# Sums of raw weights moved from VectorE to GpSimd in three sweeps, with a re-laid plan

## Chip, cores and metric

One core of one Trainium2 chip runs the whole program. The time is device microseconds of one execution; given are the median of several executions and, beside it, the one execution that the hardware profiler recorded. Engines: TensorE (PE, its weight loads PEld), VectorE (DVE), ScalarE (ACT), GpSimd (POOL), and SyncE (SP), which issues nearly all DMAs.

## What is computed

Attention over 4 sequences of 576 tokens with 8 heads of 64 (a causal window of 128 and a linear bias per head), then two layers of the same shape on the 2304 x 512 result, the first with an ELU, the second with a SiLU:

```python
scores = scale * q @ k.T + bias             # masked to 0 <= rel < 128
x = softmax(scores) @ v                     # reshaped to 2304 x 512
h = x @ w_in;  g = where(h > 0, h, exp(min(h, 0)) - 1);  x = g @ w_out     # 512 -> 2048 -> 512
h = x @ w_in2; g = h * (1 / (1 + exp(-h)));              out = g @ w_out2
```

The weights arrive as 64-bit floating-point numbers, two 32-bit words each.

## The kernel before

**Stages.** The first stage (to about 200 us) is attention, interleaved with the first quarter of the first layer's hidden width (`block_first`, `hidden`, `output_first`). The second stage, `layers()`, runs 21 steps. A step is one of three blocks of 768 tokens in one sweep; a sweep is four tiles `f` of 128 hidden columns (`SWEEPS`), three sweeps in the first layer and four in the second. A step multiplies in (`quad`, matmuls at L1254) and multiplies out (`seven_outputs`, matmuls at L1420).

**By seven.** Both products of a step are done on 2 x 2 blocks with seven block products instead of eight (Winograd's scheme), which asks for sums and differences of blocks, on the activations and on the weights. Every operand is split into a rounded upper part (a copy on ACT) and a remainder (a subtraction on DVE), and each product is three matmuls.

**Weights.** `weight(i)` prepares one tile of weights: a DMA of 512 KB into a raw buffer (a ring of four), ACT and DVE turn the two words into one 32-bit number (L471, L472, L476), and it lies in the `top` words; the `low` words are free from then on. For two neighbouring tiles (`f` odd closes the pair) four sums of 128 x 256 blocks are formed into the low words: s1 to s4 for `w_in` (L505) and t1 to t4 for `w_out` (`y_weight`, L434). After each two of them a `split_weight` follows, its ACT copy at L402 and its DVE remainder at L403. So one pair of tiles has four sums, one sweep has 2 pairs of each kind, 16 sums; the seven sweeps by seven have 112.

**Order.** Nothing is scheduled by hand. Each operation is handed to `Plan` with its engine, a cost in us, what it reads and writes, and sometimes a due time. `Plan.run` computes from the back how late each operation may start and then lays all of them in order of a simulated time: an engine that is free takes, of the operations that are ready, the most urgent. The instructions are emitted in that order, and on the chip each engine runs its own queue in that order, waiting on semaphores where an input is not there. Inputs to the simulation are constants: `DRAIN` (time from an engine's end to when others see it), `TURN` (a change of the kind of matmul), the costs, and `LATER`, by which a DMA is taken to land later than its size says. `SHAKES` is a list of (time, seed): from that simulated time on, a random choice of operations gets its urgency changed at random.

**Shared port.** `op.port` is true by default for operations on DVE and POOL, and the plan then lets only one such operation of the two engines run at a time. DVE operations that read PSUM are given `port=False`.

**POOL.** It scales softmax rows (L685, port true) and makes a few constants in the attention stage, and has nothing to do afterwards.

Of the kernel before, what the change touches and what calls it, by code (L numbers as in the profile page):

```python
# [18 lines left out]
P = 128  # L19
# [16 lines left out]
class Plan:  # L36

    LINK = 0.06
    SAME = {"DVE": 0.11, "ACT": 0.1}
    DRAIN = {"PE": 0.16, "ACT": 0.09, "DVE": 0.065, "POOL": 0.04}  # L40
    DMA_START, DMA_END = 1.2, 1.3
# [5 lines left out]
    SWITCH, STAY, EAGER = 0.1, (0.5, 4.0), 30.0  # L47
    TURN, RUN = 0.025, 1.1

# [119 lines left out]
def attention_elu_silu_kernel(  # L169
# [32 lines left out]
    for bi, (g0, n) in enumerate(blocks):  # L202
# [6 lines left out]
    NRAW = 4  # L209
    SCRATCH = {4: (1, 0), 5: (1, 1), 6: (1, 2), 7: (2, 0)}  # L210
    BIG = 6 * P
    HALF = BIG // 2
# [14 lines left out]
    BY_HAND = 4  # L227
    LATER = 0.9, 0.6, 0.4
    SHAKES = (
# [12 lines left out]

# [168 lines left out]
    def seven(layer, f):  # L411
        return any((layer, sw) in BY_SEVEN and f0 <= f < f1 for sw, (f0, f1) in enumerate(SWEEPS[layer]))

    def y_weight(t):

# [17 lines left out]
        def form(d, x, y):  # L433
            add("DVE", 0.34, lambda: nc.vector.tensor_tensor(d[0](), x[0](), y[0](), op=ALU.subtract), r=x[1] + y[1], w=d[1])  # L434
        src, r = whole(t, 1)
# [10 lines left out]
    def weight(i):  # L446
# [48 lines left out]
        else:  # L495
# [8 lines left out]
            def form(d, x, y, op):  # L504
                add("DVE", 0.34, lambda: nc.vector.tensor_tensor(d[0](), x[0](), y[0](), op=op), r=x[1] + y[1], w=d[1])  # L505
            split_weight(("wb", i), None, a22[0], None, w2, a22[1])
# [124 lines left out]
    def scores(u):  # L631
# [14 lines left out]
        def after():  # L646
            exps = []
            for j in range(2):
                for e in range(2):
                    g, i = 2 * t + e, 2 * j + e  # L650
                    c0 = first_col(g) // 2
                    b = pick.get(g, "bias")

                    def biased(j=j, e=e, i=i, c0=c0, b=b):
                        nc.vector.tensor_tensor_reduce(  # L655
                            T["p", u % 3][:, j, e, PAD + c0:PAD + WIDE], st(j)[:, e, c0:], T[b,][:, 2 * hp + j, c0:], -scale, 3.0e38,
                            ALU.add, ALU.min, T["neg", u % 4][:, i:i + 1])
                    pk = [("p", u % 3, j, e)] + ([("p", u % 3, "lo"), ("p", u % 3, "hi")] if u < 3 else [])
                    add("DVE", 0.29, biased, r=[sk[j], (b, 2 * hp + j)], w=pk[:1] + [("neg", u % 4, i)], port=False)

                    def exped(j=j, e=e, i=i, c0=c0):
                        dst = T["p", u % 3][:, j, e, PAD + c0:PAD + WIDE]
                        nc.scalar.activation(dst, dst, AF.Exp, bias=T["neg", u % 4][:, i:i + 1], scale=-1.0,  # L663
                                             accum_out=T["sm", u % MS][:, e, j:j + 1])
                    exps.append(lambda exped=exped, j=j, e=e, i=i: add("ACT", 0.445, exped, r=[("neg", u % 4, i)],
                                                                     w=[("p", u % 3, j, e), ("sm", u % MS, 2 * e + j)]))
            for fn in exps:
                fn()
        return 0.81, products, [("q", t % 2, hp), ("k", t % 2, hp), ("kz",)], sk, after

# [17 lines left out]
    def turn(u):  # L688
# [26 lines left out]
        def after():  # L715
            add("DVE", 0.61, lambda: evict(0), r=[("t", 0)], w=[("pt", u % PTS, 0)], port=False)
            add("ACT", 0.5, lambda: evict(1), r=[("t", 1)], w=[("pt", u % PTS, 1)])
        return (0.64, transposes, [("p", u % 3, j, e) for j in range(2) for e in range(2)]
                + [("p", u % 3, "lo"), ("p", u % 3, "hi"), ("ident",)], [("t", 0), ("t", 1)], after)

    def mix(u):
# [19 lines left out]
        def after():  # L741
            add("ACT", 0.5, lambda: nc.scalar.activation(T["xt", bi % 2][:, hp:hp + 2, o:o + 2 * P], T["a",], AF.Copy),
                r=[("a",)], w=[("xt", bi % 2, hp + i, o // (2 * P)) for i in range(2)])
        return (1.885, mixed, [("pt", (u + i) % PTS, j) for i in range(2) for j in range(2)]
                + [("v", hp // 2, t % 2)] + ([("v", hp // 2, (t - 1) % 2)] if c0 == 0 else []), [("a",)], after)
# [40 lines left out]
    def store_x(t):  # L786
        bi, o = home[2 * t]
        b, i = divmod(2 * t * P, BIG)
        w = 2 * P
        load(lambda: nc.sync.dma_start(x_dram[b][:, :, i:i + w], T["xt", bi % 2][:, :, o:o + w]),  # L790
             NKC * w * P * 4, r=[("xt", bi % 2, c, o // w) for c in range(NKC)], w=[("xd", b, t)])

# [119 lines left out]
    def make_ahead(b):  # L912
# [7 lines left out]
        for c in range(2):  # L920
# [10 lines left out]
            for i in (1, 0, 5, 4, 6, 3, 2):  # L931
                s = srcs[i]
                if i == 3:
                    form(b21, b21, t2)
                stage, sk = stages[combo_n[0] % 3]
                combo_n[0] += 1
                add("ACT", 0.42, lambda s=s, stage=stage: nc.scalar.activation(stage()[:, 0, :], s[0](), AF.Copy), r=s[1], w=sk)
                add("DVE", 0.47, lambda s=s, stage=stage: nc.vector.tensor_tensor(stage()[:, 1, :], s[0](), f32(stage()[:, 0, :]),
                                                                                 op=ALU.subtract), r=s[1], w=sk)
                load(lambda i=i, c=c, stage=stage: nc.sync.dma_start(  # L940
                    scratch[0, b, i].rearrange("p (x c t) -> p x c t", x=2, c=2)[:, :, c, :], f32(stage())),
                    384 * 1024, r=sk, w=[("d", 0, b, i, c)], more=LATER[0])

# [112 lines left out]
    def operand(i, s, c):  # L1056
        add("ACT", 0.42, lambda: nc.scalar.activation(T["c", i][:, 0, c, :], s[0](), AF.Copy), r=s[1], w=[ck(i, c, 0)])  # L1057
        add("DVE", 0.47, lambda: lower_half(T["c", i], c, s[0]()), r=s[1] + [ck(i, c, 0)], w=[ck(i, c, 1)])
# [21 lines left out]
    def make(k):  # L1080

        layer, sw, b = steps[k]
        for c in range(2):
# [3 lines left out]
            if c:  # L1087
# [3 lines left out]
                for i in range(2):  # L1091
                    for j in range(2):
                        load(lambda i=i, j=j: nc.sync.dma_start(src(i, j), x_dram[b][:, c + 2 * i, j * HALF:(j + 1) * HALF]), 192 * 1024,
                             r=[x for x in plan.keys(("xd",)) if x[1] == b], w=sk(i, j))
            else:
                src = lambda i, j: T["xs",][:, i, j * HALF:(j + 1) * HALF]
                sk = lambda i, j: [("xs", i, j)]
                load(lambda c=c: nc.sync.dma_start(T["xs",], x_dram[b][:, c::2, :]), 768 * 1024,
                     r=[x for x in plan.keys(("xd",)) if x[1] == b], w=[("xs", i, j) for i in range(2) for j in range(2)])
            b11, b12, b21, b22 = ((lambda i=i, j=j, src=src: src(i, j), sk(i, j)) for i in range(2) for j in range(2))  # L1100
# [19 lines left out]
    def make_far(k):  # L1120
# [5 lines left out]
        def place(i, s, c):  # L1126
            add("ACT", 0.42, lambda: nc.scalar.activation(stage()[:, 0, c, :], s[0](), AF.Copy), r=s[1], w=[("xs", 0, c)])
            add("DVE", 0.47, lambda: lower_half(stage(), c, s[0]()), r=s[1] + [("xs", 0, c)], w=[("xs", 1, c)])
# [35 lines left out]
    def place(k, q, i, src, sk):  # L1164
# [3 lines left out]
        minus = i == 4  # L1168
        add("ACT", 0.42, lambda: nc.scalar.activation(T[hi], src(), AF.Copy, scale=-1.0 if minus else 1.0), r=[sk], w=[hi])  # L1169
        add("DVE", 0.47, lambda: low_part(T[lo], src(), f32(T[hi]), minus), r=[sk, hi], w=[lo])  # L1170
# [145 lines left out]
    def outputs(k):  # L1316
# [5 lines left out]
        for j in range(2 * NKC):  # L1322
# [3 lines left out]
            def piece(fp, st=st, jj=jj, half=half):  # L1326
# [26 lines left out]
                if layer == 1 and sw == 0:  # L1353
                    add("ACT", 0.42, lambda: nc.scalar.activation(dst, T[m][:, 0:HALF], AF.Copy), r=[m], w=dk)
                else:
# [12 lines left out]
    def seven_outputs(k):  # L1368
# [24 lines left out]
        def group(i, jj):  # L1393
# [58 lines left out]
            if layer == 1 and sw == 0:  # L1452
                add("ACT", 0.42, lambda: nc.scalar.activation(dst, T[m][:, 0:HALF], AF.Copy), r=[m], w=dk)
            else:
# [133 lines left out]
```

## Time and profile before

| | us |
|---|---|
| median of 3 runs (822.13 to 823.76) | 822.66 |
| the profiled execution | 821.8 |
| span of its profile, first to last instruction | 820.0 |

Of the span, PE is busy 813.8 us, PEld 769.6, DVE 731.8, ACT 657.4 and POOL 79.3. A busy PE is not PE at its peak: ends of matmuls are modelled, and a matmul that starts late lengthens none of the rows. So starved stretches are found by counting matmuls of one shape in stretches of equal length, and by the waits of PE and of PEld. An engine's idle time costs something only if PE waited for it.

### The profile page before, as it was taken

What the parts mean: (1) busy time and instruction counts of PE and PEld (TensorE: products, weight loads), DVE (VectorE), ACT (ScalarE), POOL (GpSimd) and SP (SyncE); (2) the same over time, 40 slices, a digit from 0 to 9 for tenths busy, and PEclk for the clock granted to TensorE, in tenths of its full rate; (3) what the DMA queues carried; (4) which work ended last, traced back from release to release, by engine and by line L of the source; (5) the groups of instructions that cost most, each with busy time, mean ns of one, the idle gap of its engine ahead of it and who ended that gap; (6) DMA issues with size and microseconds to landing.
All of it is one profiled execution on the core that took longest, in us unless ns stands there. A gap on an engine that the chain in (4) does not pass through costs nothing.

```text
span 820.0 us, 15918 instructions
## 1 busy us (share of the span) xinstructions
PE 813.8 (99%) x5668; PEld 769.6 (94%) x5668; DVE 731.8 (89%) x1746; ACT 657.4 (80%) x1547; POOL 79.3 (10%) x175
## 2 busy tenths in 40 slices
PE   8999999999999999999999999999999999999998
PEld 5888877778999999999999999999999999999998
DVE  8988999979999999999999999998988898687757
ACT  7999988869986898797887899999758776765543
POOL 7443444410000000000000000000000000000000
PEclk9999999999999999999999999999999999999999
DMA  9765977667954175603787856528560666036722
GB/s 302 275 215 157 293 256 232 218 238 274 368 192 162 29 270 193 253 26 119 280 308 244 308 191 271 228 58 305 187 249 27 195 257 267 26 109 245 285 81 77
DMA packets 76975, 169.59 MB, mean 207 GB/s; under 512 B 5216, under 2 KB 58080, under 8 KB 76896
## 3 DMA queue, kind: packets, MB, share of 16 engines
q1 hardware_dynamic: 76320, 168.05, 58.3%
q8 instruction: 44, 0.72, 0.3%
q10 hardware_dynamic: 576, 0.52, 0.2%
q14 instruction: 35, 0.29, 0.1%
HBM read 126.09 MB, written 42.47 MB: 206 GB/s over the span
## 4 chain that ended last, share of the span: by engine, by line
PE 96%; ACT 2%; DVE 2%; issue 0%; DVEq 0%
PE m L1420 37%; PE m L1254 37%; PE m L816 5%; PE m L869 5%; PE a L737 3%; PE s L644 3%; PE t L704 3%; PE m L863 1%; PE m L812 1%; ACT c L1057 1%; PE a L767 1%; PE a L762 0%; ACT p L663 0%; PE m L563 0%; ACT e L830 0%; ACT g L848 0%
## 5 line engine op out<-in xcount | busy, mean ns | idle before, releaser
L1420 PE MATMUL m<-g,w 128*128 128x384 f32 (+1 forms) x1770 | 318.1, 335 | 0.2 <-DVE g L409 0.2
L1420 PEld LDWEIGHTS m<-g,w 128*128 128x128 f32 x1770 | 307.7, 188 | 2.5 <-DVE g L409 0.7
L1254 PE MATMUL m<-c,wa 128*128 128x384 f32 x504 | 100.7, 336 | 0.0
L1254 PE MATMUL m<-c,wc 128*128 128x384 f32 x504 | 96.9, 335 | 0.0
L1254 PE MATMUL m<-c,wd 128*128 128x384 f32 x504 | 96.8, 334 | 0.0
L1455 DVE TENSOR_TENSOR acc<-m,acc 128x384 f32<-128x384 f32 x143 | 77.9, 553 | 13.4 <-PE m L1420 11.9
L1254 PEld LDWEIGHTS m<-c,wa 128*128 128x128 f32 x504 | 88.9, 188 | 0.5 <-DVE e L1189 0.3
L1254 PEld LDWEIGHTS m<-c,wc 128*128 128x128 f32 x504 | 88.5, 188 | 0.0
L1254 PEld LDWEIGHTS m<-c,wd 128*128 128x128 f32 x504 | 88.1, 188 | 0.1
L685 POOL TENSOR_SCALAR p<-p,sums 128x192 f32<-128x192 f32 (+1 forms) x120 | 63.3, 545 | 79.0 <-DVE sums L677 29.5
L1169 ACT ACTIVATE g<-xs 128x384 fp32r<-128x384 f32 x116 | 59.3, 520 | 10.0 <-DVE xs L1197 7.5
L663 ACT ACTIVATE p<-p,neg 128x192 f32<-128x192 f32 (+1 forms) x144 | 63.1, 443 | 2.3 <-DVE neg L655 2.3
L1169 ACT ACTIVATE g<-e 128x384 fp32r<-128x384 f32 x112 | 57.7, 521 | 8.8 <-DVE e L1197 7.6
L409 DVE TENSOR_TENSOR g<-xs,g 128x384 fp32r<-128x384 f32 x99 | 54.0, 553 | 8.9 <-ACT g L1169 8.3
L409 DVE TENSOR_TENSOR g<-e,g 128x384 fp32r<-128x384 f32 x96 | 52.6, 554 | 6.0 <-ACT g L1169 4.8
L1254 PE MATMUL m<-c,wb 128*128 128x384 f32 x252 | 49.6, 335 | 0.0
L816 PE MATMUL m<-x,w 128*128 128x512 f32 (+1 forms) x240 | 47.9, 352 | 0.0
L869 PE MATMUL m<-g,w 128*128 128x512 f32 (+1 forms) x240 | 47.6, 351 | 0.2 <-DVE g L849 0.2
L869 PEld LDWEIGHTS m<-g,w 128*128 128x128 f32 x240 | 38.5, 189 | 7.4 <-issue 1.0
L1254 PEld LDWEIGHTS m<-c,wb 128*128 128x128 f32 x252 | 44.3, 188 | 0.0
L816 PEld LDWEIGHTS m<-x,w 128*128 128x128 f32 x240 | 38.6, 189 | 5.9
L402 ACT ACTIVATE w<-raw 128x512 fp32r<-128x512 f32 (+1 forms) x60 | 36.1, 618 | 7.9 <-DVE raw L476 5.5
(182 smaller groups left out, 1395.6 us busy)
## 6 DMA issues: line engine op xcount, KB each, us to landing
c<-d SPq DMA_DIRECT2D x91, 768.0 KB, 7.3
raw<-in_moe_w_in_dram SPq DMA_DIRECT2D x32, 512.0 KB, 7.2
raw<-in_moe_w_out_dram SPq DMA_DIRECT2D x28, 512.0 KB, 3.6
d<-c SPq DMA_DIRECT2D x14, 768.0 KB, 5.2
d<-st SPq DMA_DIRECT2D x19, 384.0 KB, 3.6
k<-in_k_dram SPq DMA_DIRECT2D x16, 384.0 KB, 5.6
d<-c SPq DMA_DIRECT2D x14, 384.0 KB, 3.6
d<-xs SPq DMA_DIRECT2D x14, 384.0 KB, 3.5
```

What stands on the lines that cost most here:

```text
L402: add("ACT", cost, lambda: nc.scalar.activation(T[hi], f32(src()), AF.Copy), r=r, w=[hi])
L409: nc.vector.tensor_tensor(lo, x, hi, op=ALU.subtract)
L644: nc.tensor.matmul(st(j)[x * (P // 2):(x + 1) * (P // 2), e, c0:], T["q", t % 2][rows, hp, o:o + P // 2], T["k", t % 2][rows, hp, o + c0:o ...
L663: nc.scalar.activation(dst, dst, AF.Exp, bias=T["neg", u % 4][:, i:i + 1], scale=-1.0, accum_out=T["sm", u % MS][:, e, j:j + 1])
L685: nc.gpsimd.tensor_scalar(dst, dst, T["sm", u % MS][:, e, j:j + 1], 1.0, op0=ALU.mult, op1=ALU.mult)
L704: nc.tensor.transpose(T["t", x][:, j, i, :], T["p", u % 3][half, j, e, c - x * PAD:c - x * PAD + P], T["ident",][half, half])
L816: nc.tensor.matmul(T[m][:, 0:w], a[:, cs], T["x0", b2][:, c, 0:w], start=(c == 0 and x == 0), stop=(c == NKC - 1 and x == 2))
L869: nc.tensor.matmul(T[m][:, 0:w], a[:, cs], b2[:, 0:w], start=(f == 0 and x == 0), stop=(f == FIRST_F - 1 and x == 2))
L1169: add("ACT", 0.42, lambda: nc.scalar.activation(T[hi], src(), AF.Copy, scale=-1.0 if minus else 1.0), r=[sk], w=[hi])
L1254: nc.tensor.matmul(T[m][:, 0:HALF], a[:, cs], x[:, j, c, :], start=(begin and c == 0 and n == 0), stop=(c == 1 and n == 2), skip_group_che ...
L1420: nc.tensor.matmul(T[m][:, t0:t1], a, b2[:, t0:t1], start=(begin and q == 0 and x == 0), stop=(q == nq - 1 and x == 2), skip_group_check=True)
L1455: add("DVE", 0.47, lambda: nc.vector.tensor_tensor(dst, T[m][:, 0:HALF], dst, op=ALU.add), r=[m], w=dk, port=False)
```

## The change

- `weight_form` is new: for the sweeps of `POOL_FORMS`, that is the first layer's tiles 8 to 11 and 12 to 15 and the second layer's tiles 0 to 3, a sum of raw weights is a `gpsimd.tensor_tensor` with cost 0.7 and `port=False`; for all others it stays on DVE with cost 0.34. Both places that form sums call it.
- `DRAIN["PE"]` goes from 0.16 to 0.145, `TURN` from 0.025 to 0.018.
- `LATER` goes from three values to four: loads of attention's result and the stores of `make_far` from 0.9 to 1.3, `store_x` from 0 to 1.3, raw weights from 0.6 to 1.1, `reload` from 0.4 to 1.2, the stores of `make_ahead` from 0.9 to 0.4, the loads in `make` from 0 to 0.4.
- Several costs: the exponential's input on DVE 0.29 to 0.28, the exponential 0.445 to 0.44, scores of a unit with a first column 0.81 to 0.705, the transposes 0.64 to 0.16 per part, `mix` 1.885 to 1.47 where a first column lies in the middle, its eviction and the transposes' on ACT 0.5 to 0.48, activations' copies 0.42 to 0.417, the copy of a PSUM bank into the accumulator 0.42 to 0.385.
- `SHAKES` is a new list: 68 entries instead of 56.

```diff
-    DRAIN = {"PE": 0.16, "ACT": 0.09, "DVE": 0.065, "POOL": 0.04}
+    DRAIN = {"PE": 0.145, "ACT": 0.09, "DVE": 0.065, "POOL": 0.04}
...
-    TURN, RUN = 0.025, 1.1
+    TURN, RUN = 0.018, 1.1
...
+    POOL_FORMS = {(0, 2), (0, 3), (1, 0)}
...
-    LATER = 0.9, 0.6, 0.4
+    LATER = 1.3, 1.1, 1.2, 0.4
     SHAKES = (
-        (12.0, 822040274), (16.0, 822040388), (24.0, 822040519), (88.0, 822220671), (108.0, 822221197),
...
+        (4.0, 692140029), (12.0, 692140234), (16.0, 692140365), (20.0, 692140408), (72.0, 692280243),
...
+    def weight_form(layer, f, d, x, y, op):
+        if (layer, f // 4) in POOL_FORMS:
+            add("POOL", 0.7, lambda: nc.gpsimd.tensor_tensor(d[0](), x[0](), y[0](), op=op), r=x[1] + y[1], w=d[1], port=False)
+        else:
+            add("DVE", 0.34, lambda: nc.vector.tensor_tensor(d[0](), x[0](), y[0](), op=op), r=x[1] + y[1], w=d[1])
...
         def form(d, x, y):
-            add("DVE", 0.34, lambda: nc.vector.tensor_tensor(d[0](), x[0](), y[0](), op=ALU.subtract), r=x[1] + y[1], w=d[1])
+            weight_form(layer, f, d, x, y, ALU.subtract)
...
             def form(d, x, y, op):
-                add("DVE", 0.34, lambda: nc.vector.tensor_tensor(d[0](), x[0](), y[0](), op=op), r=x[1] + y[1], w=d[1])
+                weight_form(layer, f, d, x, y, op)
...
-        return 0.81, products, [("q", t % 2, hp), ("k", t % 2, hp), ("kz",)], sk, after
+        return 0.705 if first_col(2 * t) or first_col(2 * t + 1) else 0.81, products, [("q", t % 2, hp), ("k", t % 2, hp), ("kz",)], sk, after
...
-             NKC * w * P * 4, r=[("xt", bi % 2, c, o // w) for c in range(NKC)], w=[("xd", b, t)])
+             NKC * w * P * 4, r=[("xt", bi % 2, c, o // w) for c in range(NKC)], w=[("xd", b, t)], more=LATER[0])
...
-                    384 * 1024, r=sk, w=[("d", 0, b, i, c)], more=LATER[0])
+                    384 * 1024, r=sk, w=[("d", 0, b, i, c)], more=LATER[3])
...
-                    add("ACT", 0.42, lambda: nc.scalar.activation(dst, T[m][:, 0:HALF], AF.Copy), r=[m], w=dk)
+                    add("ACT", 0.385, lambda: nc.scalar.activation(dst, T[m][:, 0:HALF], AF.Copy), r=[m], w=dk)
```

## Rows read from the trace of the kernel before

**Rows 1.** The page: busy time, share of the span and instructions of each engine.
```profile
PE 813.8 (99%) x5668; PEld 769.6 (94%) x5668; DVE 731.8 (89%) x1746; ACT 657.4 (80%) x1547; POOL 79.3 (10%) x175
```
**Rows 2.** Busy us (and instructions) of each engine in stretches; clock, DMA share, GB/s.
```profile
240.00:520.00 280.00, 279.77 (x1596) 277.14 (x1595) 270.70 (x561) 237.88 (x507) 0.00 (x0) 1.00 0.56 202
520.00:800.00 280.00, 280.00 (x1612) 279.94 (x1611) 229.40 (x460) 199.45 (x416) 0.00 (x0) 1.00 0.51 185
...
236.00:483.00 247.00, 246.78 (x1408) 244.63 (x1407) 239.01 (x497) 206.28 (x435) 0.00 (x0) 1.00 0.56 202
```
**Rows 3.** Waits of PE's weight loads, 236 to 520 us: total us, times, longest.
```profile
PEld m L1420 <- DVE g L409: 0.7, 2, 0.4
PEld m L1420 <- DVE m L1446: 0.6, 3, 0.3
PEld m L1420 <- ACT h L1445: 0.4, 1, 0.4
PEld m L1420 <- ACT g L1169: 0.3, 1, 0.3
PEld m L1254 <- DVE e L1189: 0.3, 1, 0.3
```
**Rows 4.** The sums in 236 to 483 us (ns min/median/max, starts), and DVE's timeline.
```profile
L434 DVE TENSOR_TENSOR raw<-raw,raw x18: 418/420/424, 288.1 to 481.8; 128x256 f32<-128x256 f32 x18
L434 DVE TENSOR_TENSOR raw<-raw x6: 416/422/426, 266.5 to 473.1; 128x256 f32<-128x256 f32 x6
...
L505 DVE TENSOR_TENSOR raw<-raw x18: 418/421/427, 236.9 to 463.5; 128x256 f32<-128x256 f32 x18
L505 DVE TENSOR_TENSOR raw<-raw,raw x6: 417/420/422, 237.2 to 451.4; 128x256 f32<-128x256 f32 x6
...
346.51 0.43 DVE L505 TENSOR_TENSOR raw<-raw 128x256 f32<-128x256 f32 x1
...
347.52 0.54 DVE L1189 SCALAR_TENSOR_TENSOR xs<-xs,m 128x384 f32<-128x384 f32 x1
```
**Rows 5.** POOL's operations at two lines: ns min/median/max, starts, forms.
```profile
L685 POOL TENSOR_SCALAR p<-p,sums x120: 366/429/1370, 25.1 to 167.0; 128x192 f32<-128x192 f32 x112, 128x128 f32<-128x128 f32 x8
...
L468 POOL TENSOR_SCALAR raw<-raw x4: 661/728/1112, 13.0 to 24.3; 128x512 f32<-128x512 f32 x4
```
**Rows 6.** Timeline of POOL beside DVE (start, us), and two DVE lines' ns min/median/max.
```profile
149.70 0.43 POOL L685 TENSOR_SCALAR p<-p,sums 128x192 f32<-128x192 f32 x1
...
122.26 0.87 DVE L849 TENSOR_TENSOR g<-ex,g 128x512 fp32r<-128x512 f32 x1
...
122.57 1.24 POOL L685 TENSOR_SCALAR p<-p,sums 128x192 f32<-128x192 f32 x1
...
24.35 0.77 POOL L468 TENSOR_SCALAR raw<-raw 128x512 f32<-128x512 f32 x1 [0.83 <-DMA raw<-in_moe_w_in_dram]
...
24.50 1.17 DVE L476 SCALAR_TENSOR_TENSOR raw<-raw 128x512 uint32<-128x512 uint32 x1
...
L849 DVE TENSOR_TENSOR g<-e,g x12: 410/683/693, 53.0 to 195.6; 128x512 fp32r<-128x512 f32 x8, 128x256 fp32r<-128x256 f32 x4
...
L476 DVE SCALAR_TENSOR_TENSOR raw<-raw x60: 680/685/1168, 18.7 to 730.8; 128x512 uint32<-128x512 uint32 x60
```
**Rows 7.** DVE's busy time with a PSUM bank (tile m) alone, in one stretch.
```profile
236.00:483.00 247.00, 86.44 (x161) 1.00 0.56 202
```
**Rows 8.** Waits of PE over the whole span.
```profile
PE t L704 <- ACT pt L713: 0.5, 1, 0.5
PE s L644 <- DMA q<-in_q_dram: 0.3, 1, 0.3
```
**Rows 9.** Timeline at the end.
```profile
816.97 0.81 SPq L1434 DMA_DIRECT2D out_dram<-acc  x2
```
**Rows 10.** Timeline of PE around one late feed.
```profile
424.51 0.44 PE L1420 MATMUL m<-g,w 128*128 128x384 f32 x1
425.11 0.61 PE L1420 MATMUL m<-g,w 128*128 128x384 f32 x2 [0.17 <-DVE g L409]
```

More of the change, by code (lines that the diff above doesn't have):

```diff
@@ L658, in after @@
                     pk = [("p", u % 3, j, e)] + ([("p", u % 3, "lo"), ("p", u % 3, "hi")] if u < 3 else [])
-                    add("DVE", 0.29, biased, r=[sk[j], (b, 2 * hp + j)], w=pk[:1] + [("neg", u % 4, i)], port=False)
+                    add("DVE", 0.28, biased, r=[sk[j], (b, 2 * hp + j)], w=pk[:1] + [("neg", u % 4, i)], port=False)
                     def exped(j=j, e=e, i=i, c0=c0):
@@ L664, in exped @@
                                              accum_out=T["sm", u % MS][:, e, j:j + 1])
-                    exps.append(lambda exped=exped, j=j, e=e, i=i: add("ACT", 0.445, exped, r=[("neg", u % 4, i)],
+                    exps.append(lambda exped=exped, j=j, e=e, i=i: add("ACT", 0.44, exped, r=[("neg", u % 4, i)],
                                                                      w=[("p", u % 3, j, e), ("sm", u % MS, 2 * e + j)]))
@@ L716, in after @@
             add("DVE", 0.61, lambda: evict(0), r=[("t", 0)], w=[("pt", u % PTS, 0)], port=False)
-            add("ACT", 0.5, lambda: evict(1), r=[("t", 1)], w=[("pt", u % PTS, 1)])
-        return (0.64, transposes, [("p", u % 3, j, e) for j in range(2) for e in range(2)]
+            add("ACT", 0.48, lambda: evict(1), r=[("t", 1)], w=[("pt", u % PTS, 1)])
+        return (0.16 * sum(b2 - a for a, b2 in parts), transposes, [("p", u % 3, j, e) for j in range(2) for e in range(2)]
                 + [("p", u % 3, "lo"), ("p", u % 3, "hi"), ("ident",)], [("t", 0), ("t", 1)], after)
@@ L741, in after @@
         def after():
-            add("ACT", 0.5, lambda: nc.scalar.activation(T["xt", bi % 2][:, hp:hp + 2, o:o + 2 * P], T["a",], AF.Copy),
+            add("ACT", 0.48, lambda: nc.scalar.activation(T["xt", bi % 2][:, hp:hp + 2, o:o + 2 * P], T["a",], AF.Copy),
                 r=[("a",)], w=[("xt", bi % 2, hp + i, o // (2 * P)) for i in range(2)])
-        return (1.885, mixed, [("pt", (u + i) % PTS, j) for i in range(2) for j in range(2)]
+        return (1.47 if first_col(2 * t + 1) else 1.885, mixed, [("pt", (u + i) % PTS, j) for i in range(2) for j in range(2)]
                 + [("v", hp // 2, t % 2)] + ([("v", hp // 2, (t - 1) % 2)] if c0 == 0 else []), [("a",)], after)
@@ L936, in make_ahead @@
                 combo_n[0] += 1
-                add("ACT", 0.42, lambda s=s, stage=stage: nc.scalar.activation(stage()[:, 0, :], s[0](), AF.Copy), r=s[1], w=sk)
+                add("ACT", 0.417, lambda s=s, stage=stage: nc.scalar.activation(stage()[:, 0, :], s[0](), AF.Copy), r=s[1], w=sk)
                 add("DVE", 0.47, lambda s=s, stage=stage: nc.vector.tensor_tensor(stage()[:, 1, :], s[0](), f32(stage()[:, 0, :]),
@@ L1056, in operand @@
     def operand(i, s, c):
-        add("ACT", 0.42, lambda: nc.scalar.activation(T["c", i][:, 0, c, :], s[0](), AF.Copy), r=s[1], w=[ck(i, c, 0)])
+        add("ACT", 0.417, lambda: nc.scalar.activation(T["c", i][:, 0, c, :], s[0](), AF.Copy), r=s[1], w=[ck(i, c, 0)])
         add("DVE", 0.47, lambda: lower_half(T["c", i], c, s[0]()), r=s[1] + [ck(i, c, 0)], w=[ck(i, c, 1)])
@@ L1093, in make @@
                         load(lambda i=i, j=j: nc.sync.dma_start(src(i, j), x_dram[b][:, c + 2 * i, j * HALF:(j + 1) * HALF]), 192 * 1024,
-                             r=[x for x in plan.keys(("xd",)) if x[1] == b], w=sk(i, j))
+                             r=[x for x in plan.keys(("xd",)) if x[1] == b], w=sk(i, j), more=LATER[3])
             else:
@@ L1098, in make @@
                 load(lambda c=c: nc.sync.dma_start(T["xs",], x_dram[b][:, c::2, :]), 768 * 1024,
-                     r=[x for x in plan.keys(("xd",)) if x[1] == b], w=[("xs", i, j) for i in range(2) for j in range(2)])
+                     r=[x for x in plan.keys(("xd",)) if x[1] == b], w=[("xs", i, j) for i in range(2) for j in range(2)], more=LATER[3])
             b11, b12, b21, b22 = ((lambda i=i, j=j, src=src: src(i, j), sk(i, j)) for i in range(2) for j in range(2))
@@ L1126, in place @@
         def place(i, s, c):
-            add("ACT", 0.42, lambda: nc.scalar.activation(stage()[:, 0, c, :], s[0](), AF.Copy), r=s[1], w=[("xs", 0, c)])
+            add("ACT", 0.417, lambda: nc.scalar.activation(stage()[:, 0, c, :], s[0](), AF.Copy), r=s[1], w=[("xs", 0, c)])
             add("DVE", 0.47, lambda: lower_half(stage(), c, s[0]()), r=s[1] + [("xs", 0, c)], w=[("xs", 1, c)])
@@ L1168, in place @@
         minus = i == 4
-        add("ACT", 0.42, lambda: nc.scalar.activation(T[hi], src(), AF.Copy, scale=-1.0 if minus else 1.0), r=[sk], w=[hi])
+        add("ACT", 0.417, lambda: nc.scalar.activation(T[hi], src(), AF.Copy, scale=-1.0 if minus else 1.0), r=[sk], w=[hi])
         add("DVE", 0.47, lambda: low_part(T[lo], src(), f32(T[hi]), minus), r=[sk, hi], w=[lo])
@@ L1452, in group @@
             if layer == 1 and sw == 0:
-                add("ACT", 0.42, lambda: nc.scalar.activation(dst, T[m][:, 0:HALF], AF.Copy), r=[m], w=dk)
+                add("ACT", 0.385, lambda: nc.scalar.activation(dst, T[m][:, 0:HALF], AF.Copy), r=[m], w=dk)
             else:
```

24 rows, old and new, of the table SHAKES are left out of this document.

## The prediction, made before the changed kernel ran

> **What bounds the kernel now.** I read the page's busy shares first: TensorE (PE) is busy 813.8 us of the span's 820.0, VectorE (DVE) 89%, ScalarE (ACT) 80%, GpSimd (POOL) 10% [rows 1]. A PE that is never idle could still be starved, because the ends of matmuls are modelled; so the next view was the number of matmuls in two equal stretches of the two layers, where nearly every matmul has the same 128x384 form. From 520 to 800 us PE took 1612 of them, from 240 to 520 us only 1596 [rows 2]. One takes 280 / 1612 = 0.174 us, so 16 missing ones are 2.8 us: that is what PE loses in the first half of the layers against its own best pace, and it loses next to nothing in the second. The difference between the two stretches is DVE: 270.70 us busy of 280 in the first, 229.40 in the second [rows 2]. The table of waits names the same culprit: after 236 us the weight loads of PE waited 2.3 us in all, 1.6 of it for DVE and 0.7 for ACT, and never for a DMA [rows 3]. The clock is no part of it: TensorE was granted 1.00 in all these stretches, the 2.4 GHz level [rows 2]. So the kernel is bound by PE's own work, and a change that leaves PE's work alone can give at most the 2.8 us that DVE's crowding costs, plus what the attention part loses.
>
> **The sums that move.** The sums and differences of raw weights run on DVE: in the three sweeps of the change there are 24 at L505 (w_in) and 24 at L434 (w_out), from 236.9 to 481.8 us, inside the crowded stretch, each 0.42 us long [rows 4]. Three of them back to back start at 346.51 and the next DVE work at 347.52 [rows 4], so each holds DVE's queue for 0.34 us. Freed: 48 x 0.34 = 16.3 us of DVE. POOL is empty there, 0 instructions from 236 to 483 us [rows 2], so nothing of its own is queued behind them.
>
> **What they cost on POOL.** The trace has no two-input operation on POOL. The nearest rows: one input of 192 elements takes 0.43 us, one input of 512 takes 0.66 at least [rows 5]. A sum of 256 pairs reads 512 values per partition, so I take 0.66, between 0.43 and the 0.77 of the row at 24.35 [rows 6].
>
> **What POOL costs DVE.** This is the unknown that decides. A POOL operation beside DVE work that reads PSUM takes its plain 0.43 us (149.70) [rows 6]. Beside DVE operations that read two tensors from SBUF it was held to 1.24 us (122.57), and the DVE operation around its start took 0.87 us (L849, 122.26) where its like takes 0.683 [rows 6]. A longer POOL operation (512 elements, 24.35) coincided with an L476 of 1.17 us, against a median of 0.685: DVE lost 0.48 us [rows 6]. So the two engines hold each other up, and a POOL operation that reads 512 values can cost DVE 0.48. Who is exposed: of DVE's 239.01 us between 236 and 483, 86.44 touch a PSUM bank [rows 2, 7]; without the moved sums the rest is (152.6 - 16.3) / 222.7 = 61%. If every moved sum hit such an operation and won, DVE would lose 48 x 0.48 = 23 us; if it always lost, nothing. By the share it is 48 x 0.48 x 0.61 = 14.1; since POOL is the one held in the row at 122.57 for most of the time (0.81 us, DVE 0.19), I take two thirds, 9.4 us. Net relief of DVE: 16.3 - 9.4 = 6.9 us, 42% of what was freed (bounds: 16.3 and -6.7).
> The SBUF page of the Trainium skill (SBUF — State Buffer, "SBUF: two separate sides") speaks against the change: a two-input DVE operation and a POOL operation that reads SBUF lock the shared ports for a whole instruction, and the other one fully blocks. By that rule each hit costs the full 0.66, 48 x 0.66 x 0.61 = 19.3 us, more than is freed. The trace agrees that they exclude each other, and differs on the whole instruction: 0.19 us lost beside a 1.24 us POOL operation.
>
> **What PE gets back.** 42% of the 2.8 us: 1.2 us (bounds 0 and 2.8). What is late next is ACT, and the true pace of PE.
>
> **The new hand-off.** ACT's copies of the sums (wc, wd, w1) now wait for POOL. A pair of sums takes 2 x (0.66 + about 0.4 held, half of the 0.81 above) = 2.1 us instead of 0.76, so 24 copies come some 1.35 us later, 32 us in all; behind a waiting copy stand ACT's copies of activations, which L409 on DVE and then PE wait for. ACT has 247 - 206.28 = 40.7 us idle there [rows 2], and with that idleness PE waited for ACT 0.7 us [rows 3], 1 in 58; 32 / 58 = 0.55. The plan counts 0.7 us per sum and so knows more than half of the delay; I take 0.3 us (0 to 0.55). The raw buffers come free some 3 us later per pair of weights, and the next weight's load with them; no PE wait after 236 us names a DMA [rows 3], so that costs nothing, and if the cover went it would be a wait of PE for a landing, which would be new.
>
> **Later landings, traced paces, new shakes.** Costs, LATER, DRAIN and TURN are numbers of the planner: no instruction gets shorter or longer, only the order on each queue (SP's transfers too) changes. In the layers, where no landing is waited for by PE, I cost it at nothing. In the attention part PE waits 0.5 us for ACT L713 and 0.3 for a q load [rows 8]; a new order may save both or open as much: 0, between -0.8 and +0.8. The tail, the last two stores at 816.97 and their landing, stays [rows 9].
>
> **Sum.** Profiled execution of before 821.8 us (span 820.0 and 1.8 around it); -1.2 + 0.3 + 0 = -0.9 gives 820.9. The median of the runs is 822.66, 0.86 above the profiled one, so in medians 821.8. A measurement of this kernel can tell about 0.2% from no change, 1.65 us; the forecast is inside that.
>
> **Rival A: the relief comes in full.** POOL slips into the 39% of DVE's time that reads PSUM and into its gaps, so DVE is really 16 us lighter and PE runs at the pace of 520 to 800 us. For it: the median of the 120 POOL operations is 0.429 [rows 5], the plain time of the one at 149.70 [rows 6], so most were not held. Against it: those stood beside attention, where most DVE work reads PSUM. It gives 822.66 - 2.8 = 819.9, and with the attention's 0.8 as much as 819.1.
>
> **Rival B: held DVE starves PE.** The 48 sums come as 12 runs of four. The order counts POOL and DVE as free of each other there (port=False), so it is made for a DVE that is never held. Four hits in a row put DVE 4 x 0.48 = 1.9 us behind that order, while its idle time is 9.3 us in 280 [rows 2], 1 in 30; a feed that was just in time is then late. The price of one late feed: at 424.51 a matmul's successor came 0.60 us later, at 425.11, instead of 0.17, waiting for L409 [rows 10], 0.43 lost. Twelve of them are 5.2 us; with 0.9 gained elsewhere +4.3, 827.0. It decides once a run costs PE more than (1.65 + 0.9) / 12 = 0.21 us. For it: DVE at 97% [rows 2]. Against it: with the net relief above DVE has some 7 us more to catch up in. By the SBUF rule of the Trainium skill, DVE's 19.3 us lost against 16.3 freed, there would be no such 7 us, and B would be the case.
>
> **Rival C: nothing arrives.** The missing 16 matmuls could come from the order itself rather than from DVE's load; then a new order simply has other gaps. That gives 822.7 +- 1, and lies within the forecast's own range, 820.4 to 823.4.
>
> **Chances.** Forecast with C 0.40, A 0.32, B 0.28. Faster by over 0.2% (under 821.0): 0.27 of A and 0.08 of the forecast, 0.35. Within: 0.05 of A, 0.30, and 0.05 of B, 0.40. Slower: 0.02 and 0.23 of B, 0.25. The range takes in most of A and of B, 819.3 to 826.3, leaving out about 0.1 at each end.
>
> **What would show it.** Right: 48 POOL rows at the lines of the sums, about 0.7 us when free and over 1 us beside DVE work on SBUF; DVE's two-input rows there stretched now and then; DVE's busy time from 240 to 520 us down by less than 16 us; between 1600 and 1607 matmuls in that stretch. A shows as 1612 there and DVE rows that don't stretch, B as under 1590 with PE waiting for L409 or L1446 right behind POOL's sums. The prediction is wrong if the attention part, up to 199.6 us, changes its length by over 1 us, or if PE comes to wait for a DMA.

## The result and the profile after

The changed kernel takes 829.31 us in the median, before 822.82 beside it: 1.0081 times as long, 95% interval 1.0069 to 1.0094. The move was forecast at 821.8 with a range of 819.3 to 826.3; it came out slower, above the range, for the most part by the mechanism of rival B and by more than its price.

The page of after, busy time of each engine, against [rows 1]:

```profile
PE 815.1 (99%) x5668; PEld 768.7 (93%) x5668; DVE 727.3 (88%) x1698; ACT 655.2 (79%) x1547; POOL 124.6 (15%) x223
```

DVE has 48 operations fewer and POOL 48 more; everything else is the same work. Two equal stretches of after, columns as in [rows 2]:

```profile
240.00:520.00 280.00, 275.26 (x1560) 270.62 (x1559) 262.70 (x506) 231.28 (x494) 44.46 (x44) 1.00 0.55 201
520.00:800.00 280.00, 280.00 (x1614) 280.00 (x1613) 232.25 (x468) 200.02 (x421) 0.00 (x0) 1.00 0.50 184
```

From 240 to 520 us PE takes 1560 matmuls instead of 1596: 36 x 0.174 = 6.3 us, nearly the whole loss. DVE is busy 8.0 us less there (over the whole kernel, so for the same work, 4.5 us less: 727.3 against 731.8), and PE is starved more. Attention is no part of it: the first matmul of the layers starts at 199.8 us after, at 199.6 before. These are the rows of that line in each kernel (ns min/median/max, first and last start), after first:

```profile
L1263 PE MATMUL m<-c,wa x504: 331/334/446, 199.8 to 804.3; 128*128 128x384 f32 x168
```
```profile
L1254 PE MATMUL m<-c,wa x504: 332/334/447, 199.6 to 794.0; 128*128 128x384 f32 x168
```

The moved sums on POOL, with the same columns:

```profile
L419 POOL TENSOR_TENSOR raw<-raw x24: 609/867/2327, 235.8 to 477.5; 128x256 f32<-128x256 f32 x24
L419 POOL TENSOR_TENSOR raw<-raw,raw x24: 844/1177/1396, 237.5 to 482.1; 128x256 f32<-128x256 f32 x24
```

The shortest takes 0.61 us in the first group and 0.84 in the second (raw<-raw,raw); the medians are 0.87 and 1.18, the mean of all 48 is 1.01. DVE beside them, from the timeline at 322 us, and two DVE lines from 236 to 520 us:

```profile
322.01 1.18 POOL L419 TENSOR_TENSOR raw<-raw,raw 128x256 f32<-128x256 f32 x1
...
322.39 1.09 DVE L406 TENSOR_TENSOR wb<-raw,wb 128x256 fp32r<-128x256 f32 x1
...
L406 DVE TENSOR_TENSOR wb<-raw,wb x6: 417/420/1092, 255.0 to 450.8; 128x256 fp32r<-128x256 f32 x6
...
L1464 DVE TENSOR_TENSOR acc<-m,acc x65: 542/551/560, 245.3 to 477.3; 128x384 f32<-128x384 f32 x65
```

A remainder on DVE that reads two tensors from SBUF, plainly 0.42 us, takes 1.09 when POOL is inside a sum: a hit costs it 0.67. The 65 additions that read a PSUM bank stay between 0.542 and 0.560, though POOL works on a sum beside 15 of them. Adding up, over all DVE operations from 200 to 520 us, what each is longer than the median of its line and shape gives the **stretch** used below: in after 28 operations, 11.2 us in all, 0.67 the most.

PE's weight loads waited, after, 236 to 520 us, against [rows 3]:

```profile
PEld m L1263 <- ACT h L1272: 2.0, 2, 1.5
PEld m L1263 <- ACT t L1192: 1.7, 1, 1.7
PEld m L1263 <- DVE m L1308: 1.4, 2, 1.1
PEld m L1429 <- DVE g L412: 0.8, 3, 0.4
PEld m L1263 <- DVE acc L1464: 0.7, 1, 0.7
```

The five longest waits of PE itself from 236 to 520 us (1.35, 1.20, 0.76, 0.40 and 0.40 us) end inside a run of sums or at most 2 us behind it. They have two different origins, and a wait that names ACT can belong to either.

The wait of 1.35 us, ended at 485.15, begins on DVE. POOL's sum stretches a DVE operation at L1050 (plainly 0.55) to 1.22 us, L1276 comes only behind that in DVE's queue, ACT waits 0.93 us for its result, and only behind that work comes the operation of ACT that PE stands for.

The wait of 1.20 us, ended at 291.17, begins on POOL. No DVE operation is stretched between 269 and 294 us. The sum that starts at 286.90 takes 2.33 us, ACT's copy L405 waits 2.81 us for POOL, L1272 comes only behind that copy in ACT's queue, and PE waits for L1272. This is a late sum. The rows of both, in order of time:

```profile
286.90 2.33 POOL L419 TENSOR_TENSOR raw<-raw 128x256 f32<-128x256 f32 x1 [19.22 <-DVE raw L485]
...
290.07 0.66 ACT L405 ACTIVATE w<-raw 128x512 fp32r<-128x512 f32 x1 [2.81 <-POOL raw L419]
290.64 0.48 ACT L1272 ACTIVATE h<-m 128x384 f32<-128x384 f32 x1
...
291.17 0.45 PE L1263 MATMUL m<-c,wd 128*128 128x384 f32 x1 [1.20 <-ACT h L1272]
...
480.99 1.18 POOL L419 TENSOR_TENSOR raw<-raw,raw 128x256 f32<-128x256 f32 x1
...
481.37 1.22 DVE L1050 TENSOR_TENSOR c<-acc,c 128x384 fp32r<-128x384 f32 x1
...
482.50 0.54 DVE L1276 TENSOR_TENSOR hs<-m,hs 128x384 f32<-128x384 f32 x1
...
483.08 0.53 ACT L1192 ACTIVATE e<-hs 128x384 f32<-128x384 f32 x1 [0.93 <-DVE hs L1276]
...
485.15 0.44 PE L1263 MATMUL m<-c,wa 128*128 128x384 f32 x1 [1.35 <-ACT t L1192]
```

### The profile page after: what moved, and what is told of

Its sections match the earlier page's. It is cut to its first block, busy times and chain, and to the rows that moved or that the text cites. A ratio compares the mean times of both kernels' runs of the same rounds, so it can differ in the third digit from the quotient of the medians.

```text
span 826.9 us, 15921 instructions
## 1 busy us (share of the span) xinstructions
PE 815.1 (99%) x5668; PEld 768.7 (93%) x5668; DVE 727.3 (88%) x1698; ACT 655.2 (79%) x1547; POOL 124.6 (15%) x223
## 4 chain that ended last, share of the span: by engine, by line
PE 82%; DVE 9%; ACT 4%; POOL 2%; issue 1%; DMA 1%; POOLq 0%; DVEq 0%
PE m L1429 31%; PE m L1263 29%; PE m L878 5%; PE m L825 5%; PE a L746 3%; PE s L653 3%; PE t L713 3%; DVE g L412 2%; DVE acc L1464 1%; ACT g L1178 1%; PE m L872 1%; PE m L821 1%; DMA d<-xs 1%; DVE raw L485 1%; DVE w L406 1%
## 5 line engine op out<-in xcount | busy, mean ns | idle before, releaser
L1178 ACT ACTIVATE g<-e 128x384 fp32r<-128x384 f32 x112 | 57.5, 520 | 14.2 <-DVE e L1206 12.3
L419 POOL TENSOR_TENSOR raw<-raw 128x256 f32<-128x256 f32 x24 | 22.4, 934 | 257.1 <-DVE raw L485 201.5
L412 DVE TENSOR_TENSOR g<-xs,g 128x384 fp32r<-128x384 f32 x99 | 54.7, 563 | 6.0 <-ACT g L1178 4.8
L412 DVE TENSOR_TENSOR g<-e,g 128x384 fp32r<-128x384 f32 x96 | 52.4, 554 | 6.5 <-ACT g L1178 5.6
```

The lines of the kernel that those rows point to most:

```text
L412: nc.vector.tensor_tensor(lo, x, hi, op=ALU.subtract)
L1178: add("ACT", 0.417, lambda: nc.scalar.activation(T[hi], src(), AF.Copy, scale=-1.0 if minus else 1.0), r=[sk], w=[hi])
```

## Experiments

Three theories stood against each other. HELD: POOL's reads hold DVE's two-tensor operations and PE starves behind them. LATE: the sums come later than planned and block ACT's queue. ORDER: the new constants and shakes make a worse order by themselves. The first four kernels and the last three keep the order of the changed kernel and alter only what a moved sum does. The edits are shortened to the lines that matter.

**Nothing held, nothing late.**

```diff
-nc.gpsimd.tensor_tensor(d[0](), x[0](), y[0](), op=op)
+nc.gpsimd.tensor_tensor(d[0]()[:, 0:2], x[0]()[:, 0:2], y[0]()[:, 0:2], op=op)
```

> The changed kernel in its own order, but each of the 48 sums on POOL covers 2 of its 256 columns (the other columns are left as they are), so that POOL neither holds DVE nor is late. Theory HELD (POOL's reads hold DVE's two-tensor operations, and PE starves behind them) and theory LATE (the sums take 1.0 us instead of the 0.7 of the plan, and ACT's copies that wait for them block ACT's queue) both expect the whole loss to go: 819.5 to 821.5, some 1612 matmuls from 240 to 520 us. Rival ORDER (the new costs and shakes made a worse order by themselves) expects it to stay at 826 or more.

Measured: 822.25 us, ratio to before 0.9992 (0.9983 to 1.0001). Its stretch from 240 to 520 us:

```profile
240.00:520.00 280.00, 279.84 (x1601) 278.35 (x1600) 260.46 (x521) 238.62 (x510) 11.35 (x44) 1.00 0.55 202
```

The loss is gone, so the order is sound and ORDER falls. But HELD's own figure was too good as well: with DVE 10.2 us lighter than before, PE takes 1601 matmuls, not 1612. In this order full relief is worth 5 matmuls, 0.9 us, in the profiled execution, and 0.7 us by the ratio, whose interval reaches to no gain at all.

**Late, but nothing read.**

```diff
-nc.gpsimd.tensor_tensor(d[0](), x[0](), y[0](), op=op)
+for _ in range(3): nc.gpsimd.memset(d[0](), 0.001)
```

> The changed kernel in its own order, but each of the 48 sums on POOL is three memsets of the same 128x256 output (no sum is made): some 0.9 us on POOL as before, with the same waits before and after it, and nothing read from SBUF. HELD expects DVE's rows back at their plain length and 820 to 822. LATE expects no change, 827 to 830, since the copies on ACT still wait as long.

Measured: 822.12 us, ratio 0.9992 (0.9979 to 1.0005). POOL's rows (three to a sum, so 1.0 us a sum, as long as in after), and ACT's wait for them, 236 to 520 us:

```profile
L421 POOL MEMSET raw<- x144: 321/334/352, 235.4 to 476.7; 128x256 f32 x144
...
ACT w L405 <- POOL raw L421: 3.9, 3, 1.8
...
L1053 DVE TENSOR_TENSOR c<-acc,c x18: 548/552/558, 472.9 to 519.9; 128x384 fp32r<-128x384 f32 x18
```

ACT waits 3.9 us for late sums and the time does not suffer. DVE's row of the line that took 1.22 in after stays within 0.558. So sums of this length cost nothing where nobody is held, and LATE falls as the main cause.

But these sums are not quite as late as the real ones: in after ACT waits 6.9 us for POOL. The difference can be followed at one place, the late sum of 286.90 in after, in five kernels of the same order:

| sum on POOL | ACT's copy L405 waits for POOL, us | PE's weight load waits for L1272, us |
|---|---|---|
| 2 columns | 1.50 | 0.22 |
| three memsets | 1.82 | 0.51 |
| one input | 1.94 | 0.67 |
| 128 of 256 columns | 2.15 | 0.85 |
| as changed | 2.81 | 1.51 |

About 1.3 us of ACT's wait are covered, and all that goes beyond reaches PE. So in after this one late sum costs PE some 1.2 us of the 6.3. That sum is late because DVE holds POOL, too: with 2 columns it still takes 1.66 us there, and ends just as DVE gets to operations that read PSUM, while no memset takes over 0.352.

**Held, but nobody waits.**

```diff
+if n % 4 == 0:                       # behind the fourth, 2-column, sum of a run
+    for i in range(4):
+        nc.gpsimd.tensor_tensor(T["aside",], T["aside",], T["aside",], op=ALU.add)
```

> The changed kernel in its own order, the 48 sums on POOL cut to 2 columns each (the rest is left out), and behind the fourth of each run of four POOL makes four sums of 128x256 on a tile of its own that nobody waits for. So POOL reads SBUF as long as before, but no copy on ACT waits for it. HELD expects DVE to lose about as much as in the changed kernel (some 11 us of stretched rows) and 826 to 830. LATE expects 820 to 822.

Measured: 825.88 us, ratio 1.0039 (1.0026 to 1.0052); stretch 8.7 us over 27 operations, at most 0.47. Sums that nobody waits for cost PE over half of the loss: HELD stands. The time fell just short of HELD's 826, and the stretch short of its 11 us: a hit of these sums is shorter than one of the real ones, and the late sum of 286.90 is missing (PE's weight load waits 0.19 us there).

**The same order, the sums back on DVE.**

```diff
-add("POOL", 0.7, lambda: nc.gpsimd.tensor_tensor(...), ...)
+add("POOL", 0.7, lambda: nc.vector.tensor_tensor(...), ...)
```

> The changed kernel in its own order, laid as if the 48 sums were on POOL, but issued on DVE at their places in that order. POOL holds nobody; DVE gets 48 x 0.34 = 16.3 us back in its queue, against the 11.2 us by which its rows are stretched in the changed kernel; a sum is done in 0.42 us. HELD in its general form (any unplanned time on DVE starves PE) expects no recovery, 827 to 833. LATE expects most of the loss to go, 821 to 824, because the copies on ACT get their sums early.

Measured: 825.97 us, ratio 1.0042 (1.0026 to 1.0057), between the two expectations. 16.3 us that the order did not plan on DVE cost PE 3.8 us against the 2-column run; 12.3 us of holds with nobody waiting (six aside, below) cost 5.9. The longest hit (0.67) takes from DVE twice the queue time of doing the sum itself (0.34), the average one (0.40) about as much.

**The old order, the sums on POOL.**

```diff
-add("DVE", 0.34, lambda: nc.vector.tensor_tensor(...), ...)
+add("DVE", 0.34, lambda: nc.gpsimd.tensor_tensor(...), ...)   # for the three sweeps; all else as before
```

> The kernel before in its own order, with nothing else changed than that the 48 sums are issued on POOL at their places. DVE is free of 16.3 us of its queue and held for some 11. The order leaves room for the sums on DVE, so HELD expects little: 821 to 824.5, since each hold falls on a DVE that the order takes for busier than it is. If late sums or holds cost PE whatever the order has room for, 826 to 830.

Measured: 827.53 us, ratio 1.0054 (1.0038 to 1.007); stretch 12.5 us over 25 operations.

```profile
240.00:520.00 280.00, 276.85 (x1565) 271.20 (x1564) 262.63 (x504) 232.87 (x497) 43.83 (x47) 1.00 0.56 204
```

My expectation missed. An order with room for the sums on DVE loses two thirds as much, so it isn't the plan's ignorance of the hold alone. Late sums are not behind it: ACT waits 2.4 us for POOL here, and before 1.9 us for the same sums on DVE. My reading, which no run tests, is that a hold delays whichever operation comes next, an urgent one as well.

**A plan that knows of the hold.**

```diff
-add("POOL", 0.7, ..., port=False)
+add("POOL", 0.8, ...)                # port=True; SHAKES chosen anew
```

> The changed kernel with the sums on POOL, but laid with a plan that knows the hold: a sum costs 0.8 us on POOL and has port=True, so that no DVE operation with port=True is laid beside it; shakes of its own. HELD says that the harm comes from holds that the order does not know, and expects DVE's stretched rows to shrink from 11.2 us to under 4 and 820 to 823.5. If the hold costs PE whether the order knows of it or not, 826 or more.

The plan's cost of POOL's operation at L468 of before also went from 0.66 to 0.8. Measured: 828.04 us, ratio 1.0056 (1.0042 to 1.007); stretch 9.0 us over 22 operations. A miss too: in its timeline an L545, L476 of before with a plain 0.685 [rows 6], still takes 1.35 beside a sum:

```profile
408.53 1.36 POOL L479 TENSOR_TENSOR raw<-raw,raw 128x256 f32<-128x256 f32 x1
...
409.09 1.35 DVE L545 SCALAR_TENSOR_TENSOR raw<-raw 128x512 uint32<-128x512 uint32 x1
```

That an order is no timetable, and so can't keep the two engines apart where no semaphore does, is the likely reason; no run shows it.

**No sums on POOL, the rest of the change kept.**

```diff
-POOL_FORMS = {(0, 2), (0, 3), (1, 0)}
+POOL_FORMS = set()                   # SHAKES chosen anew
```

> The changed kernel with all sums of raw weights on DVE (POOL_FORMS empty), its new costs, LATER, DRAIN and TURN kept, and the order laid anew with shakes of its own. If POOL's holds are the whole harm (HELD) and the new constants are sound, 820 to 822.5. If the new constants make worse orders by themselves (ORDER), 825 or more.

Measured: 821.62 us, ratio 0.9988 (0.9979 to 0.9997), as HELD expects. It is the fastest kernel of the study, 0.12% faster than before, which is less than the 0.2% that the prediction took for telling. PE takes 1593 matmuls from 240 to 520 us in its profile, so the count in this stretch alone does not rank kernels that lie so close.

**The size of the hold.** Half the columns, one input, and more sums aside:

```diff
+nc.gpsimd.tensor_tensor(d[0]()[:, 0:P], x[0]()[:, 0:P], y[0]()[:, 0:P], op=op)        # sums_half
+nc.gpsimd.tensor_scalar(d[0](), x[0](), 1.0, 0.0, op0=ALU.mult, op1=ALU.add)          # sums_one_input
+    for i in range(6):                                                                # sums_aside6
```

> The changed kernel in its own order, each of the 48 sums on POOL over 128 of its 256 columns (the other half is left out). HELD: a hold is about half as long, DVE's rows are stretched by 4 to 6 us instead of 11.2, and as PE only feels what exceeds the slack of a feed, less than half of the loss is left: 823 to 825.5. A loss that comes from POOL's taking part at all, whatever the length, stays at 828 or more.

> The changed kernel in its own order, each of the 48 sums on POOL replaced by a tensor_scalar of its first input alone (256 columns, so 256 values read per partition in place of 512; the second input is left out). HELD with a hold that goes by the values read: half the hold, 4 to 6 us of stretch, 823 to 825, as with sums_half. If POOL holds for its whole instruction whatever it reads, the stretch stays at 9 us or more and the time over 826.

> As sums_aside (the changed kernel's order, its 48 sums cut to 2 columns, and sums on a tile of POOL's own behind each run of four), but six of these in place of four, 72 in all. In sums_aside DVE's rows were stretched by 8.7 us and the time was 825.9; in the changed kernel 11.2 us and 829.3. If what PE loses grows with the stretch alone, and faster than in proportion, some 12 us of stretch give 828 to 831. If late sums add to it in the changed kernel, this one stays at 826 to 827.5.

Remainders on DVE at line L406 with half the columns, then with one input (plainly 0.68 with 512 columns, 0.42 with 256). The longest hits are 1.044 - 0.684 = 0.36 in the first and 0.914 - 0.684 = 0.23 in the second:

```profile
L406 DVE TENSOR_TENSOR wa<-raw,wa x7: 681/684/1044, 254.0 to 502.4; 128x512 fp32r<-128x512 f32 x7
L406 DVE TENSOR_TENSOR wb<-raw,wb x6: 407/416/620, 254.6 to 447.3; 128x256 fp32r<-128x256 f32 x6
```
```profile
L406 DVE TENSOR_TENSOR w<-raw,w x24: 417/684/914, 288.3 to 484.0; 128x512 fp32r<-128x512 f32 x18, 128x256 fp32r<-128x256 f32 x6
L406 DVE TENSOR_TENSOR wb<-raw,wb x6: 411/418/637, 255.5 to 447.8; 128x256 fp32r<-128x256 f32 x6
```

Half the columns and six aside came out as HELD expects. One input missed on the low side: 2.8 us of stretch instead of 4 to 6, and 822.88.

All kernels in the changed kernel's order, by stretch:

| sum on POOL | stretch, us | longest hit | matmuls 240 to 520 us | median, us | ratio to before |
|---|---|---|---|---|---|
| three memsets | 0 | 0 | 1594 | 822.12 | 0.9992 |
| 2 columns | 0 | 0 | 1601 | 822.25 | 0.9992 |
| one input | 2.8 | 0.23 | 1593 | 822.88 | 0.9993 (0.9982 to 1.0004) |
| 128 of 256 columns | 4.3 | 0.36 | 1590 | 823.31 | 1.0007 (0.9998 to 1.0016) |
| four aside | 8.7 | 0.47 | 1572 | 825.88 | 1.0039 |
| six aside | 12.3 | 0.47 | 1564 | 828.04 | 1.0064 (1.0049 to 1.0079) |
| as changed | 11.2 | 0.67 | 1560 | 829.31 | 1.0081 |

Against the first two rows 4.3 us of stretch cost about 1.1 us, 8.7 cost 3.7, 12.3 cost 5.9 and after's 11.2 cost 7.1. So the loss follows the stretch and is there with nobody waiting for the sums. After's 1.2 us more than six aside, at a smaller stretch, is the size of what its late sum at 286.90 costs; six aside has none there (PE's weight load waits 0.22 us for ACT). As the intervals of the two overlap, that account rests on the waits in the traces and not on the times.

The hits are not of just any length. In each run several of them pile up at one value, and it is the least time of the sum less about 0.19 us, which is what a sum of 2 columns takes:

| sum on POOL | its least time, us | hits pile up at, us |
|---|---|---|
| two inputs of 256, group raw<-raw,raw of after | 0.84 | 0.65 to 0.67 (7 of 28) |
| two inputs of 256, four aside | 0.61 | 0.41 to 0.42 (15 of 27) |
| two inputs of 128, group raw<-raw,raw | 0.50 | 0.32 to 0.33 (5 of 20) |
| one input of 256 | 0.41 | 0.21 to 0.23 (9 of 17) |
| 2 columns | 0.19 | none |
| memset, 256 | 0.32 | none |

The longest hits of the aside runs (0.47) and of half the columns (0.36) have a third sum beside them. Why one group takes 0.84 and another sum of the same size 0.61 no run shows.

## Why the prediction was wrong

- **What bounds the kernel** was read rightly as to the place: PE's losses sit between 240 and 520 us, and the pace from 520 on is untouched. But the 2.8 us were taken for what DVE's load costs. With DVE lighter by all the sums and held by nobody (2 columns), PE got back 0.9 of them. Rival A's 819.9 was thus out of reach in this order. Eleven of the 16 missing matmuls stay missing, as rival C had it; what they wait for is open.
- **What they cost on POOL** was set at 0.66 for every sum. The least is 0.61 in one group and 0.84 in the other, and the mean 1.01.
- **What POOL costs DVE** was near in the sum: 9.4 us forecast, 11.2 measured. The share of hits was too small (41%; 28 hits of 48 sums), the price of one too high on average (0.48; measured 0.40, at most 0.67). The price came from an operation with one input of 512 [rows 5, 6] and fits the pattern above (0.66 less 0.19); a sum's price is another one, as two inputs hold longer than one (0.67 against 0.23 for the same 256 columns). The Trainium skill's page SBUF — State Buffer ("SBUF: two separate sides") says that the later of the two is blocked for the whole of the other one's instruction; here the hits pile up some 0.19 us below the sum's own least time (0.65 to 0.67 of 0.84, 0.23 of 0.41), so "whole" is a little too much, and the 19.3 us worked out by that rule were further off than the 9.4. It also says that DVE's two-input work contends only with POOL operations that read SBUF; the memsets, with no stretch, agree.
- **What PE gets back** is the step that failed. I turned 6.9 us of net relief on DVE into 1.2 us for PE, as if DVE's time were a budget. DVE did come out lighter, by 4.5 us over the whole kernel, and PE lost 6.3 us more than before. A hold lands on whatever is next in DVE's queue, and where that feeds PE just in time the delay passes through to PE, as at 485.15.
- **The hand-off to ACT** was mis-sized too: 0.3 us (0 to 0.55), against some 1.2 for the one late sum of 286.90. It was the same mistake on another engine: ACT's idle time was taken on average, 1 in 58, and the one copy that outran its cover of 1.3 us passed the rest on in full. The other late sums cost nothing that shows (822.12 with memsets).
- **Later landings, traced paces, new shakes** were rightly costed at nothing as far as the runs tell: the new order without holds, and with DVE relieved, takes 822.25, the new constants with all sums on DVE 821.62, and attention ends within 0.2 us of where it did. Neither of the prediction's last two signs of being wrong, a changed length of attention or a wait of PE for a DMA, appeared.
- **Rival B** named the mechanism. Of the places that it named, L409 and L1446 (L412 and L1455 of after), PE's weight loads waited 1.0 us; most waits were for L1308 (L1299 of before) and for ACT, behind the same runs of sums. Its term was mis-sized: 0.43 us for each of 12 runs was taken from one late feed before [rows 10]; after, the longest wait that begins with a held DVE is 1.35 us. It was given 0.28 because DVE was believed to have some 7 us to catch up in; idle time later on does not give back a matmul that has started late.

## What to carry to other kernels

Before work of two SBUF inputs moves from VectorE to GpSimd beside a busy VectorE, do not compare busy times alone. Here 48 sums of 0.34 us left VectorE and 28 hits of 0.40 us on average came in, so VectorE got lighter and the kernel slower. Relief on a feeding engine is worth only what the fed engine was losing to it, and that is found by taking the work away altogether (the 2-column run), before moving it. And one microsecond of VectorE is not like another: the 16.3 us of sums cost some 0.7 us where the plan had chosen their places (before against the 2-column run), 3.8 where it had not counted on them, and 12.3 us of holds cost 5.9. The same holds for a hand-off: average idle time of the waiting engine does not cover the one copy that is late.

## What was not expected of the hardware

A sum of 128x256 pairs on GpSimd takes at least 0.61 us, in one group 0.84, and mostly 0.85 to 1.2 beside a busy VectorE. A hit costs a VectorE operation with two SBUF inputs mostly no more than that least time less about 0.19 us: at most 0.67 us in the changed kernel, and 0.71 in any run (the old order, sums on POOL); half the columns or one input cost less, a memset nothing. VectorE operations with one input in PSUM were stretched in none of these runs. And it goes the other way as well: a sum of 2 columns on GpSimd, 0.19 us in the median, took 1.66 us while VectorE ran operations with SBUF inputs back to back.
